# Splitting the second weight's pairs 3 to 7 inside the main loop instead of ahead of it

## The chip, the core and the metric

The kernel runs on one core of one Trainium2 chip. The metric is device time in microseconds (us), from the program's start to its end. Names used below: TensorE is PE in the profile, VectorE is DVE, ScalarE is ACT, GpSimd is POOL, SyncE is SP.

## The reference

A block-sparse attention is followed by a two-layer network with a gate. All tensors are float32.

```python
# q, k, v: 4 batches, 8 heads, 768 positions, 64 per head
scores = q @ k.T / sqrt(64)
# mask in blocks of 32: neighbours, first and last block, 3 sampled blocks per block
attn = softmax(where(mask, scores, -1e9))
x = (attn @ v) as rows: 3072 tokens x 512
h = x @ w_in                                  # 512 x 2048
g = h * erf(softplus(h))
out = g @ w_out                               # 2048 x 512
```

## The kernel before

**How the work is tiled.** Attention is cut into units: for each batch 11 "m" units of two query blocks each and 4 "f" units for the first and last block (one per pair of heads). The network works on chunks of 256 tokens in 8 groups of 256 hidden columns each; one group of one chunk is a step `m` of the main loop (line 987). In step `m`:

- TensorE does, in this order, the value products of an older unit (`values`, tile `po`), the first product of group `m` (`ff_first`, tile `h`), the scores of the newest unit (`scores`, tile `s`), and the second product of group `m - 3` (`ff_second`, tile `o`).
- ScalarE does the logarithms and squares of group `m` (`ff_logs`, tiles `x` and `y`), a first half of the attention result (`turn`), the exponentials of the newest unit (`soft_exp`: four to `pf`, then one copy to `p`), and the exponential of group `m` (`ff_exp`, `y<-y`).
- VectorE does the gate of group `m - 2` (`ff_gate`: `y<-y,h`, then the two halves of `g`), the low half of the last unit's probabilities (`soft_low`, tile `p`), the norm of the older unit (`norm`, tiles `rinv` and `xf`), the maximum of the newest unit (`soft_max`, tile `less`), the second half of the result (`turn`), and one step of the polynomial of group `m` (`ff_power`, `y<-y,x`).

Some steps carry no unit. In the first chunk, steps 0, 1, 3, 4, 5 and 6 have one, steps 2 and 7 do not. Four units have their maximum and exponentials done before the main loop's list begins, and the work before it is laid out by a scheduler; from step 3 on (`held[0] = m >= FF_LAG`, line 989) every engine runs its instructions in the order in which the code lists them. SP and POOL follow the listed order throughout.

**Buffers that couple the engines.** `h` has three PSUM buffers, so the first product of group `m` needs the gate of group `m - 3` done. `po` has one: the value products need the norm of the unit before them done. `s` has one: scores need the exponentials of the unit before done. `vn`, the scaled values of the next batch on their way to memory, has one buffer: the ScalarE instruction that fills it for the second time waits until the first transfer has left it. `qm`, the ordered queries for the "f" units, is written by VectorE in step 5 and read by the scores of step 6.

**The second weight.** All float32 factors are multiplied as two float16 halves. The second weight `w_out` lies in tile `wo` as 16 slices of 128 rows, in 8 pairs; group `fg` of the second product reads pair `fg`. Making the halves of a pair takes two instructions on ScalarE (`high`, line 466: scale and round) and then two on VectorE (`low`, line 470: what the rounding left). They are the rows `wo<-wo,sums` below. The generator `weights` (line 527) does this for pair `n - 9` in its rounds 9 to 16, all of which run before the main loop's list begins; the scheduler has laid them among the first two or three steps.

Of the kernel before, what the change touches and what calls it, by code (L numbers as in the profile page):

```python
# [31 lines left out]
def sparse_attention_moe(ctx: ExitStack, tc: tile.TileContext, qT, kT, v, sampled, w_in, w_out, out):  # L32
# [32 lines left out]
    NF = DFF // P  # L65
# [9 lines left out]
    PV_LAG = 3  # L75
    GATE_LAG = 2
    FIRST, SEEN = 6, 4
    assert NR == 3 and NB == 24 and D == 64 and H == 8

    def pick(n, share):  # L80
# [352 lines left out]
    def decode(key, i):  # L433

        first = i + APART[key]
        t = wi if key == "i" else wo
        w32 = t[:, first : first + 2, :].rearrange("p n c -> p (n c)")
        parts = [raw for n in (i, i + 1) for raw in places.pop((key, n), [])]
        mag = mags[(i // 2) % 2]
        c = 0  # L440
        for raw in parts:
            w = raw.shape[1] // 2
            raw = raw.rearrange("p (n w) -> p n w", w=2)
            lo, hi = raw[:, :, 0], raw[:, :, 1]
            m = mag[:, c : c + w]
            dve.tensor_scalar(m, hi, 3, 0x3FFFFFFF, ALU.logical_shift_left, ALU.bitwise_and)
            dve.scalar_tensor_tensor(m, hi, -0x40000000, m, ALU.bitwise_and, ALU.bitwise_or)
            done = w32[:, c : c + w].bitcast(I32)
            dve.scalar_tensor_tensor(done, lo, 29, m, ALU.logical_shift_right, ALU.bitwise_or)
            c += w  # L450

    def square(key, i):
        first = i + APART[key]
        w32 = (wi if key == "i" else wo)[:, first : first + 2, :].rearrange("p n c -> p (n c)")
        sq = mo.tile([P, 512], F32, tag="s", name=f"sq_{key}{i}", bufs=3).bitcast(BF16)
        act.activation(sq, w32, AF.Square, accum_out=wsq[key][:, i // 2 : i // 2 + 1])

    def halves(key, i):
        t, t16 = (wi, wi16) if key == "i" else (wo, wo16)
        return t[:, i + APART[key], :], t16[:, i, :512], t16[:, i, 512:]  # L460

    def scale_of(key, i):
        n = i // (2 * NK) if key == "i" else i // 2
        return (si if key == "i" else so)[:, n : n + 1]

    def high(key, i):
        w32, hi16, _ = halves(key, i)
        act.activation(hi16, w32, AF.Copy, scale=scale_of(key, i))

    def low(key, i):  # L470
        w32, hi16, lo16 = halves(key, i)
        dve.scalar_tensor_tensor(lo16, w32, scale_of(key, i), hi16, ALU.mult, ALU.subtract)
# [17 lines left out]
    def scale_pair(i):  # L490
        n = i // 2
        total = ps_o.tile([P, DM], F32, tag="o", name=f"total_{i}")[:, :1]
        pe.matmul(total, ones, wsq["o"][:, n : n + 1], start=True, stop=True)
        scale_part(total, n)

    def bound_part(part):
        return pow2_bound(wsq["i"][:, part * NK : (part + 1) * NK], f"wi{part}", True)

    def scale_half(total, part):
        scale_part(total, NP + part)  # L500
        dve.tensor_scalar(diag, eye, si[:, part : part + 1], None, ALU.mult)

    def ratios():
        dve.tensor_reduce(least[:, 0:1], si, AX.X, ALU.min)
        dve.tensor_scalar(rest_i, ii, least[:, 0:1], 2.0**-H_SHIFT, ALU.mult, ALU.mult)
        dve.tensor_reduce(least[:, 1:2], so, AX.X, ALU.min)
        for part in range(2):
            c = slice(part * NP // 2, (part + 1) * NP // 2)
            dve.tensor_scalar(ratio[:, c], io[:, c], least[:, 1:2], rest_i[:, part : part + 1], ALU.mult, ALU.mult)
        dve.tensor_scalar(least.bitcast(I32), least.bitcast(I32), -1.0, 254 * unit23, ALU.mult, ALU.add)  # L510
        dve.tensor_tensor(unscale, least[:, 0:1], least[:, 1:2], ALU.mult)
# [3 lines left out]
    def rest(i):  # L515
        rests[i] = ps_o.tile([P, DM], F32, tag="o", name=f"rest_{i}")
        pe.matmul(rests[i], diag, halves("i", i)[0], start=True, stop=False)

    def rest_low(i):
        pe.matmul(rests[i], less16, halves("i", i)[1], start=False, stop=True)  # L520

    def rest_out(i):
        act.activation(halves("i", i)[2], rests.pop(i), AF.Copy)

    assert NK * NG == NF == 16

    def weights():
        loads = {5: (("o", 0),), 6: (("o", 2),), 7: (("o", 4), ("o", 6)), 10: (("o", 8),), 11: (("o", 10),)}
        sum_i = None
        for n in range(17):  # L530
            key, i = "io"[n // 8 % 2], n % 8 * 2
            if n in (4, 9):
                with tc.high_priority():
                    scale_half(sum_i, n // 8)
            pair = None
            if 5 <= n < 9:
                pair = 2 * (n - 5)
            if 10 <= n < 14:
                pair = 2 * (n - 6)
            if pair is not None:  # L540
                for part in range(2):
                    rest(pair + part)
                    high("i", pair + part)
            if n < 16:
                decode(key, i)
            if pair is not None:
                for part in range(2):
                    rest_low(pair + part)
                    rest_out(pair + part)
            if n < 16:  # L550
                square(key, i)
            if n >= 9:
                i = 2 * (n - 9)
                scale_pair(i)
                high("o", i)
                high("o", i + 1)
                low("o", i)
                low("o", i + 1)
            for piece in loads.get(n, ()):
                load_w(*piece)  # L560
            if n in (3, 7):
                sum_i = bound_part(n // 4)
            yield
        ratios()
# [214 lines left out]
    def ff_exp(b, ch, fg):  # L779
        y = ffs[b, ch, fg][1]  # L780
        act.activation(y, y, AF.Exp, bias=C4 * C2 * C2, scale=-C4)
# [73 lines left out]
    def ahead(m):  # L855

        for c in range(1, B):
            if m - v_from[c] == 2:
                load_v(c, 1)
# [28 lines left out]
    def seen(unit):  # L888

        if unit[0] == "m":  # L890
            return unit[1], unit[2], None
        if unit[2] % 2 == 1:
            return unit[1], NU, unit[2] // 2
        return None
# [6 lines left out]
    def used_values(place):  # L901
        nonlocal vfree
        if place[2] is None:
            vfree += 2
        elif place[2] == 1:
            vfree += 3

    def unit_of(n):
        return units[n] if 0 <= n < len(units) else None
# [77 lines left out]
    for m in range(len(groups) + FF_LAG):  # L987
        ch, i = divmod(m, NGR)
        held[0] = m >= FF_LAG
        if m > FF_LAG:  # L990
            for u in range(CT):
                ff_store(*groups[m - FF_LAG - 1], u)
        steps = 0
        if ch < len(until):
            first = until[ch - 1] if ch else FIRST
            steps = int(i in spread[until[ch] - first])
        elif begun < len(units) + PV_LAG:
            steps = 1
        assert steps in (0, 1)
        group = groups[m] if m < len(groups) else None  # L1000
        last = groups[m - GATE_LAG] if GATE_LAG <= m < len(groups) + GATE_LAG else None
        unit = unit_of(begun) if steps else None
        old = unit_of(begun - PV_LAG) if steps and begun - PV_LAG >= SEEN else None
        place = seen(old) if old else None
        begun += steps
        if unit:
            ahead(begun - 1)
        if place:
            values(*place)
            used_values(place)  # L1010
        if group:
            ff_first(*group)
            ff_logs(*group)
        if steps:
            gathers()
        if unit:
            scores(unit)
            used_keys(unit)
        if m >= FF_LAG:
            for u in range(CT):  # L1020
                ff_second(*groups[m - FF_LAG], u)
        if last:
            ff_gate(*last)
        low_v()
        if open_unit:
            soft_low(open_unit)
        if place:
            norm(*place)
        if unit:
            soft_max(unit)  # L1030
        if place:
            turn(*place)
        if group:
            ff_power(*group)
        if unit:
            soft_exp(unit)
        if group:
            ff_exp(*group)
        open_unit = unit
        if unit:  # L1040
            next_queries(begun - 1)
            behind(begun - 1)
# [38 lines left out]
```

## Time and profile before

| | us |
|---|---|
| median of 3 runs | 765.58 (760.46 to 772.68) |
| profiled execution | 764.91 |
| its span | 763.1 |
| TensorE busy in the span | 686.3 (90%) |
| ScalarE busy | 591.9 (78%) |
| VectorE busy | 575.4 (75%) |
| GpSimd busy | 201.6 (26%) |

The profiled execution's own time is 1.8 us more than its span and lies between the runs. Busy time is a sum over stages that differ: the loop's first dozen steps, from about 120 to 200 us, are read below by single instructions. In these rows a time is the start from the span's beginning, then the length; a bracket gives the idle time of that engine just before and what ended it. Lengths of neighbours on one engine overlap by about a tenth of a microsecond, so a spacing of starts is a little shorter than a length.

### The profile page before, as it was taken

Reading aid. Unit: us, or ns where it says so; the run is one execution under the profiler, and the core shown is the slowest. Engines: PE = TensorE matmul, PEld = TensorE weight load, DVE = VectorE, ACT = ScalarE, POOL = GpSimd, SP = SyncE. Lnnn points to the kernel's source line nnn. Section 1 sums busy time; section 2 is a strip of 40 time slices with the busy share of each in tenths; the row PEclk is TensorE's granted clock in tenths of the full one; section 3 lists DMA queues with packets and bytes.
Section 4 is the critical chain, followed back from the end, with each engine's and each line's share of the span. In section 5 each row is a group of like instructions: output and inputs, shape, how many; then the busy total and the mean of one; then the engine's idle time right before and its main releaser. Section 6 shows DMA issues by size and latency. Waiting matters only on the chain.

```text
span 763.1 us, 24883 instructions
## 1 busy us (share of the span) xinstructions
PE 686.3 (90%) x10400; PEld 450.6 (59%) x10400; DVE 575.4 (75%) x1122; ACT 591.9 (78%) x1023; POOL 201.6 (26%) x413
## 2 busy tenths in 40 slices
PE   1336887998999999999999999999999999999997
PEld 0213554655655666666566666666666666667663
DVE  6983999978777788778687878787777786665453
ACT  2544999878877887878888887888788887776774
POOL 3026624303364313130533312033433120000000
PEclk9976998998999999999999999999999999999999
DMA  8999835896599999855997799938988677130000
GB/s 304 415 293 283 257 91 119 195 224 154 136 224 211 193 208 182 212 144 87 250 191 162 187 166 194 251 89 185 223 157 182 130 147 168 29 77 2 8 29 27
DMA packets 188048, 129.36 MB, mean 170 GB/s; under 512 B 137760, under 2 KB 160928, under 8 KB 186912
## 3 DMA queue, kind: packets, MB, share of 16 engines
q1 hardware_dynamic: 173584, 84.50, 54.1%
q10 hardware_dynamic: 8464, 25.43, 10.4%
q0 software_dynamic: 5888, 17.84, 9.6%
q8 instruction: 81, 1.33, 0.7%
q14 instruction: 31, 0.25, 0.1%
HBM read 82.81 MB, written 12.95 MB: 125 GB/s over the span
## 4 chain that ended last, share of the span: by engine, by line
PE 78%; DMA 6%; DVE 5%; ACT 5%; issue 3%; SPq 2%; ACTq 0%; DVEq 0%
PE h L48 31%; PE o L48 31%; PE s_m L48 7%; PE po_None L48 4%; PE s_f L48 3%; SPq L48 2%; DMA vbuf<-vtab 2%; DMA wo<-in_w_in_dram 2%; DMA vtab<-vn 1%; ACT x L48 1%; PE po L48 1%; DVE room L48 1%; DMA vbuf<-in_v_dram 1%; ACT pf_m L48 1%; DVE less_m L48 1%
## 5 line engine op out<-in xcount | busy, mean ns | idle before, releaser
L48 PE MATMUL h<-xT,wi 128*128 128x256 f16 x2304 | 272.3, 275 | 5.0 <-DVE y L48 4.5
L48 PE MATMUL o<-wo,g 128*128 128x512 f16 x1152 | 264.5, 379 | 0.5 <-DVE g L48 0.2
L48 PEld LDWEIGHTS <-wi 128*128 128x128 f16 x2304 | 223.7, 99 | 45.8 <-DVE y L48 4.6
L48 ACT ACTIVATE x<-x 128x512 f32<-128x512 f32 x288 | 181.6, 631 | 8.9
L48 PEld LDWEIGHTS <-g 128*128 128x128 f16 x1152 | 109.5, 98 | 127.4 <-issue 6.6
L48 POOL DMA_INDIRECT vbuf<-vtab,idx x88 | 96.5, 1097 | 185.1 <-PE po_None L48 130.3
L48 DVE SCALAR_TENSOR_TENSOR y<-y,x 128x512 f32<-128x512 f32 x96 | 67.1, 699 | 95.0 <-ACT x L48 91.6
L48 POOL COPY kbuf<-kx 128x128 f32 (+1 forms) x280 | 87.3, 357 | 94.4 <-PE s_m L48 79.8
L48 ACT ACTIVATE x<-h,isg 128x512 f32<-128x512 f32 x96 | 65.4, 682 | 49.2 <-PE h L48 31.9
L48 ACT ACTIVATE y<-y 128x512 f32<-128x512 f32 x96 | 59.7, 622 | 32.9 <-DVE y L48 32.9
L48 ACT ACTIVATE pf_m<-s_m,less_m 128x256 f32<-128x256 f32 x176 | 68.9, 473 | 19.7 <-DVE less_m L48 18.7
L48 DVE SCALAR_TENSOR_TENSOR g<-y,sums,g 128x512 f16<-128x512 f32 x96 | 73.1, 762 | 3.4
L48 DVE SCALAR_TENSOR_TENSOR y<-y,h 128x512 f32<-128x512 f32 x96 | 65.2, 679 | 0.1
L48 ACT ACTIVATE y<-x 128x512 f32<-128x512 f32 x96 | 60.4, 631 | 3.0
L48 DVE TENSOR_REDUCE less_m<-s_m 128x4 f32<-128x1024 f32 x44 | 53.6, 1218 | 11.7 <-PE s_m L48 11.6
L48 PEld LDWEIGHTS <-pT_m 128*32 128x32 f16 x3168 | 35.4, 98 | 33.9 <-issue 31.4
L48 PE MATMUL po_None<-vbuf,pT_m 128*32 128x65 f16 (+2 forms) x3168 | 41.9, 205 | 13.2 <-issue 12.5
L48 PE MATMUL s_m<-kbuf,qt 64*32 64x160 f32 x1408 | 48.2, 316 | 3.7 <-issue 2.8
L48 DVE TENSOR_SCALAR g<-y,sums 128x512 f16<-128x512 f32 x96 | 48.0, 500 | 3.4
L48 PE MATMUL s_m<-kx,qt 64*32 64x96 f32 x1408 | 31.6, 259 | 20.4 <-ACT kx L48 13.3
L48 DVE SCALAR_TENSOR_TENSOR p_m<-pf_m,p_m 128x1024 f16<-128x1024 f32 x38 | 46.4, 1221 | 0.3 <-issue 0.3
L48 DVE TENSOR_TENSOR x<-xf,x 128x256 f16<-128x256 f32 x44 | 18.8, 426 | 31.7 <-ACT x L48 31.6
(110 smaller groups left out, 609.8 us busy)
## 6 DMA issues: line engine op xcount, KB each, us to landing
vbuf<-vtab SPq DMA_DIRECT2D x80, 195.0 KB
vraw<-in_v_dram ACTq DMA_DIRECT2D x9, 768.0 KB
vtab<-vn SPq DMA_DIRECT2D x16, 390.0 KB
vbuf<-vtab SPq DMA_DIRECT2D x12, 520.0 KB
wo<-in_w_out_dram ACTq DMA_DIRECT2D x6, 1024.0 KB
qt<-in_qT_dram SPq DMA_DIRECT2D x20, 256.0 KB
kr<-in_kT_dram ACTq DMA_DIRECT2D x12, 384.0 KB
vbuf<-vtab SPq DMA_DIRECT2D x32, 130.0 KB
```

The source lines that it names most:

```text
L48: done = call(*args, **kwargs)
```

## The change

A constant `LATE = 3` divides the eight pairs. Pairs 0 to 2 are split where they were. For pairs 3 to 7 the two `high` and two `low` instructions are taken out of the generator and listed at the end of steps 4 to 8 of the main loop, behind `ff_exp` and ahead of `next_queries` and `behind`. The pair split at the end of step `m` is `m - 1`, which the second product reads in step `m + 2`. The scales of the pairs (`scale_pair`) stay in the generator. Nothing is computed more or less often.

```diff
+    LATE = 3
...
+    def convert(pair):
+        for n in (2 * pair, 2 * pair + 1):
+            high("o", n)
+        for n in (2 * pair, 2 * pair + 1):
+            low("o", n)
...
                 scale_pair(i)
-                high("o", i)
-                high("o", i + 1)
-                low("o", i)
-                low("o", i + 1)
+                if i < 2 * LATE:
+                    convert(i // 2)
...
         if group:
             ff_exp(*group)
+        if LATE <= m - 1 < NF // 2:
+            convert(m - 1)
         open_unit = unit
```

ScalarE ahead of step 3, before: from the rounding of the first weight's last slices (`wi`) to the exponential of group 0 (`y_0_0<-y_0_0`). `x_0_0` and `x_0_1` belong to groups 0 and 1, `pf_m_7` to the newest unit.

```order
L48 ACTIVATE wi<-rest_1149 128x512
L48 ACTIVATE wo<-wo,sums 128x512 x2
L48 ACTIVATE x_0_0_1417<-h_0_0_1392,isg_1390 128x512
...
L48 ACTIVATE x_0_0_1417<-x_0_0_1417 128x512
L48 ACTIVATE wo<-wo,sums 128x512 x2
L48 ACTIVATE pf_m_7_1653<-s_m_7_1601,less_m_7_1644 128x256 x2
L48 ACTIVATE x_0_1_1571<-x_0_1_1571 128x512
L48 ACTIVATE pf_m_7_1653<-s_m_7_1601,less_m_7_1644 128x256 x2
L48 ACTIVATE y_0_0_1421<-y_0_0_1421 128x512
```

The same place in the changed kernel:

```order
L48 ACTIVATE wi<-rest_1145 128x512
L48 ACTIVATE x_0_0_1397<-h_0_0_1372,isg_1370 128x512
...
L48 ACTIVATE pf_m_7_1633<-s_m_7_1581,less_m_7_1624 128x256 x4
L48 ACTIVATE y_0_1_1555<-x_0_1_1551 128x512
L48 ACTIVATE x_0_0_1397<-x_0_0_1397 128x512
L48 ACTIVATE p_m_7_1638<-pf_m_7_1633 128x4x256
L48 ACTIVATE x_0_1_1551<-x_0_1_1551 128x512
L48 ACTIVATE y_0_0_1401<-y_0_0_1401 128x512
```

Two pairs of `wo` are gone ahead of the exponential of group 0, and the copy `p_m_7` of the newest unit, which stood behind it, now stands ahead of it.

VectorE at the same place, before: `y_0_0`, `y_0_1` and `g_0_0` belong to groups 0 and 1, `p_m_7` to the newest unit.

```order
L48 TENSOR_TENSOR sums<-sums 128x1
L48 SCALAR_TENSOR_TENSOR y_0_0_1421<-y_0_0_1421,h_0_0_1392 128x512
L48 TENSOR_SCALAR g_0_0_1696<-y_0_0_1421,sums 128x512
L48 SCALAR_TENSOR_TENSOR wo<-wo,sums 128x512
L48 SCALAR_TENSOR_TENSOR g_0_0_1696<-y_0_0_1421,sums,g_0_0_1696 128x512
L48 SCALAR_TENSOR_TENSOR wo<-wo,sums 128x512
L48 SCALAR_TENSOR_TENSOR p_m_7_1658<-pf_m_7_1653,p_m_7_1658 128x4x256
L48 SCALAR_TENSOR_TENSOR wo<-wo,sums 128x512 x4
```

The same place in the changed kernel:

```order
L48 TENSOR_TENSOR sums<-sums 128x1
L48 SCALAR_TENSOR_TENSOR y_0_0_1401<-y_0_0_1401,x_0_0_1397 128x512
L48 SCALAR_TENSOR_TENSOR p_m_7_1638<-pf_m_7_1633,p_m_7_1638 128x4x256
L48 SCALAR_TENSOR_TENSOR y_0_1_1555<-y_0_1_1555,x_0_1_1551 128x512
L48 SCALAR_TENSOR_TENSOR y_0_0_1401<-y_0_0_1401,h_0_0_1372 128x512
L48 TENSOR_SCALAR g_0_0_1676<-y_0_0_1401,sums 128x512
L48 SCALAR_TENSOR_TENSOR g_0_0_1676<-y_0_0_1401,sums,g_0_0_1676 128x512
```

All the `wo` rows have left this place (ten in the whole stretch), and `p_m_7` and the step of group 1 stand ahead of the gate of group 0.

VectorE and ScalarE at the end of step 4, in the changed kernel, VectorE first (from the maximum of unit 9 to the gate of group 3), then ScalarE (from the exponentials of unit 9 to group 5):

```order
L48 TENSOR_REDUCE less_m_9_2078<-s_m_9_2019 128x4
L48 TENSOR_SCALAR less_m_9_2078<-less_m_9_2078 128x4
L48 TENSOR_TENSOR x_0_6_2081<-xf_6_2074,x_0_6_2081 128x256
L48 SCALAR_TENSOR_TENSOR y_0_4_1993<-y_0_4_1993,x_0_4_1989 128x512
L48 SCALAR_TENSOR_TENSOR wo<-wo,sums 128x512 x2
L48 TENSOR_REDUCE vmax_1641<-vraw_1_1684 128x1
L48 TENSOR_REDUCE top_v_2099<-vmax_1641 128x1
L48 SCALAR_TENSOR_TENSOR y_0_3_1788<-y_0_3_1788,h_0_3_1759 128x512
```

```order
L48 ACTIVATE pf_m_9_2086<-s_m_9_2019,less_m_9_2078 128x256 x4
L48 ACTIVATE p_m_9_2091<-pf_m_9_2086 128x4x256
L48 ACTIVATE y_0_4_1993<-y_0_4_1993 128x512
L48 ACTIVATE wo<-wo,sums 128x512 x2
L48 DMA kr_0_2103<-in_kT_dram 128x768
L48 ACTIVATE x_0_5_2203<-h_0_5_2178,isg_1370 128x512
```

Only the `wo` rows are new at this place; without them the rows of before are the same in the same order. Steps 5, 6, 7 and 8 take theirs at the same point. The lists of POOL and SP are unchanged.

## Rows read from the trace of the kernel before

**Rows 1.** Part 1 of the page: busy time, share, instructions.

```profile
PE 686.3 (90%) x10400; PEld 450.6 (59%) x10400; DVE 575.4 (75%) x1122; ACT 591.9 (78%) x1023; POOL 201.6 (26%) x413
```

**Rows 2.** Stretches: window, length, PE, PEld, DVE, ACT, POOL, granted clock, DMA, GB/s.

```profile
120.00:130.00 10.00, 6.72 (x89) 4.65 (x90) 9.13 (x20) 10.00 (x20) 1.75 (x3) 0.66 0.36 80
...
300.00:500.00 200.00, 198.59 (x3027) 132.20 (x3020) 157.91 (x301) 167.53 (x287) 51.95 (x111) 1.00 0.90 185
```

**Rows 3.** Timeline of TensorE, steps 3, 4, 6 and 9: start, length, instruction.

```profile
123.28 5.30 PE L48 MATMUL h<-xT,wi 128*128 128x256 f16 x24 [4.50 <-DVE y L48]
...
129.82 2.76 PE L48 MATMUL o<-wo,g 128*128 128x512 f16 x12
134.39 0.88 PE L48 MATMUL po_None<-vbuf,pT_m 128*32 128x65 f16 x72 [1.80 <-issue]
135.21 2.79 PE L48 MATMUL h<-xT,wi 128*128 128x256 f16 x24
...
150.00 0.89 PE L48 MATMUL po_None<-vbuf,pT_m 128*32 128x65 f16 x72 [0.68 <-DVE xf L48]
...
174.72 1.50 PE L48 MATMUL po_None<-vbuf,pT_m 128*32 128x65 f16 x72 [4.18 <-issue]
176.15 4.72 PE L48 MATMUL h<-xT,wi 128*128 128x256 f16 x24
```

**Rows 4.** Instructions that touch `wo`, 112 to 132 us: nanoseconds min/median/max.

```profile
L48 DVE SCALAR_TENSOR_TENSOR wo<-wo,sums x10: 741/752/803, 115.0 to 129.8; 128x512 f16<-128x512 f32 x10
L48 ACT ACTIVATE wo<-wo,sums x9: 750/769/785, 111.4 to 129.0; 128x512 f16<-128x512 f32 x9
```

**Rows 5.** Timeline of VectorE: norm of unit 5, in step 3.

```profile
133.74 0.55 DVE L48 TENSOR_REDUCE xf<-po_None 128x192 f32<-128x384 f32 x1
```

**Rows 6.** Timeline of ScalarE: one pair's `high`; ends of steps 4 to 7.

```profile
118.64 1.36 ACT L48 ACTIVATE wo<-wo,sums 128x512 f16<-128x512 f32 x2
...
145.59 0.61 ACT L48 ACTIVATE y<-y 128x512 f32<-128x512 f32 x1
146.11 0.67 ACT L48 ACTIVATE x<-h,isg 128x512 f32<-128x512 f32 x1
...
154.70 0.61 ACT L48 ACTIVATE y<-y 128x512 f32<-128x512 f32 x1
...
162.49 0.61 ACT L48 ACTIVATE y<-y 128x512 f32<-128x512 f32 x1
...
171.67 0.63 ACT L48 ACTIVATE y<-y 128x512 f32<-128x512 f32 x1 [0.83 <-DVE y L48]
```

**Rows 7.** Timeline of VectorE, steps 4 to 8: gates, and what follows each power.

```profile
137.00 0.68 DVE L48 SCALAR_TENSOR_TENSOR y<-y,h 128x512 f32<-128x512 f32 x1
...
143.80 1.75 DVE L48 TENSOR_REDUCE vmax<-vraw 128x1 f32<-128x1536 f32 x1
...
145.66 0.68 DVE L48 SCALAR_TENSOR_TENSOR y<-y,h 128x512 f32<-128x512 f32 x1
...
152.89 0.58 DVE L48 COPY qm<-qt 64x256 f32<-64x256 f32 x2
...
154.01 0.68 DVE L48 SCALAR_TENSOR_TENSOR y<-y,h 128x512 f32<-128x512 f32 x1
...
161.58 0.68 DVE L48 SCALAR_TENSOR_TENSOR y<-y,h 128x512 f32<-128x512 f32 x1
...
166.82 1.22 DVE L48 SCALAR_TENSOR_TENSOR vn<-vraw,s_v,vn 128x384 f16<-128x384 f32 x2 [3.25 <-ACT vn L48]
...
171.56 0.68 DVE L48 SCALAR_TENSOR_TENSOR y<-y,h 128x512 f32<-128x512 f32 x1
```

**Rows 8.** Two transfers out of `vn`: SP's issue and who waited for the landing.

```profile
157.12 0.36 SPq L48 DMA_DIRECT2D vtab<-vn  x1
...
166.11 1.12 ACT L48 ACTIVATE vn<-vraw,s_v 128x384 f16<-128x384 f32 x2 [3.01 <-DMA vtab<-vn]
...
168.10 0.36 SPq L48 DMA_DIRECT2D vtab<-vn  x1
...
172.57 0.25 POOL L48 MEMSET vn<- 128x24 f16 x1 [1.47 <-DMA vtab<-vn]
```

## The prediction

> **What bounds the kernel now.** I read the page's busy times first, then a table of stretches, then the timelines of TensorE, VectorE and ScalarE over 110 to 200 us. Over the whole span TensorE is busy 90% [rows 1], and from 300 to 500 us it is busy 198.6 of 200 us [rows 2]: there TensorE is the end, nothing in the change touches it, and a delay of TensorE before 200 us is carried nearly whole to the end. So the change is worth what it does to TensorE's arrival at about step 10.
>
> The reader should see three holes in TensorE in the loop's first steps [rows 3]. The first product of step 3 starts after 4.50 us idle that VectorE's gate of group 0 ended, and runs 5.30 us, twice its later 2.79. The value products of step 4 start after 1.80 us idle; the profile gives no releaser, but the norm of unit 5 frees their only buffer and its reading of `po` ends at 133.74 + 0.55 = 134.29 [rows 5], 0.10 before the start at 134.39. Third, 4.18 us idle before step 9's value products at 174.72, again behind a late norm: VectorE had stood 3.25 us for ScalarE's `vn`, and ScalarE 3.01 us for the transfer that left `vn` [rows 7, 8].
>
> **What the change removes.** Ten ScalarE and ten VectorE instructions of 0.77 and 0.75 us [rows 4] (the sample shows nine of ScalarE's, the trace misses one) leave the stretch 111 to 131 us; with the overlap of neighbours that is about 6.2 us of ScalarE and 6.6 of VectorE. What it buys:
>
> - Step 3's start. Two of ScalarE's pairs (2.5 us) stood ahead of the exponential of group 0, but the copy `p_m_7` (about 1.0) now stands there, and on VectorE `p_m_7` (1.1) and the step of group 1 (0.7) now stand ahead of the gate. Laying ScalarE's list out from 110.95 I get `p_m_7` ready at 120.5, then 1.1 + 0.7 + 0.7 on VectorE: the gate is done at about 123.0 instead of 123.2. Gain 0.3 us; the slow first product stays, since TensorE stands idle as long.
> - Step 4's start. VectorE no longer has eight `low` ahead of the norm of unit 5, which ends near 128.6, while TensorE's `o` of step 3 ends at 129.82 + 2.76 - 0.3 = 132.3. The 1.80 us hole closes. TensorE enters step 4 at 132.3 instead of 134.39: **gain 2.1 us**.
> - VectorE's own lead is larger: the maximum of unit 8 can start with its scores at 129.6 instead of behind the backlog at 134.6, less a new wait of 0.8 for ScalarE. Its gate of step 4 comes at 132.9 instead of 137.00 [rows 7]: a lead of 4.1.
>
> **What it adds.** Two instructions on each of ScalarE and VectorE per step look cheap. The place makes them dear. In the new order VectorE's two `low` stand right behind `y<-y,x`, and each waits for ScalarE's `high`, which stands behind four exponentials, the copy `p` and the exponential of the group. All of VectorE's list behind them waits too: the next gate, `soft_low`, the norm. I read the stall off the rows of before, as if the pair stood there, with 1.3 us for two `high` [rows 6] and 0.7 for the last `low` [rows 4]:
>
> - Step 4: ScalarE's exponential is done at 146.11 [rows 6]; 146.11 + 1.3 + 0.7 = 148.1, where VectorE went on at 143.80 [rows 7]. 4.3 us, of which 1.3 is work.
> - Step 5: 154.70 + 0.5 + 2.0 = 157.2 against 152.89: 4.3 us.
> - Step 6: 162.49 + 0.5 + 2.0 = 165.0 against 161.58: 3.4 us.
> - Step 7: 171.67 + 0.5 + 2.0 = 174.2 against 171.56: 2.6 us.
> - Step 8: the same kind, but behind it stands the norm for a value product of step 12, since steps 10 and 11 have none; cost nothing. If that cover is gone it costs up to 2.6.
>
> Now the running balance of VectorE against the rows of before. It enters step 4 with 4.1 in hand; 0.6 goes to a wait for ScalarE, whose logarithms lead only by TensorE's 2.1; the stall takes 4.3: 0.8 behind at the gate of 145.66. About 0.3 comes back in the norm of unit 7, which ran slow before. Step 6's value products, 150.00 before, come at about 150.7 while TensorE is ready at 147.3: a new hole of some 3.4 us, and the gain of 2.1 is gone. Step 5's stall makes it 4.6 to 4.8 behind at 154.01, and `qm` (152.89 to 153.5 before) comes at about 158, so step 6's scores wait as well. Step 6's stall makes it 8.0 behind at 161.58; but the next instruction had waited 3.25 us [rows 7], so the delay there is 4.7 again.
>
> The transfer from `vn` decides the next bit. It was issued at 157.12 and let ScalarE go on at 166.11, 9.0 us; another, at 168.10, was gone by 172.57, 4.5 us [rows 8]. The issue moves to about 161.8. With 9.0 us ScalarE passes it at 170.8, with 4.5 at once behind its `high`, at 168.9. Group 7's logarithms follow, and VectorE's step on them (170.88 before) is 4.1 or 2.6 late; with step 7's stall of about 2.5 the norm of unit 9 and step 9's value products are **6.6 or 5.1 late**. The shorter transfer is the nearer, as fewer loads are left ahead of it: I take 5.5, and keep both. From step 10 on TensorE waits for nothing new: the gates it needs come 3 us or more before it. Pair 3's halves are ready near 145 and read near 159, so the weights themselves are never late. SP and POOL keep their lists; their waits on VectorE move with it.
>
> Sum: 5.5, less about 0.5 that holes of TensorE after 200 us may take back (bounds 0 and 1), is +5 on the profiled execution's 764.9: **770 us**. That execution lies 0.7 below the median of the runs.
>
> **The clock.** The new hole before step 6 is 3.4 us. After the 4.50 us hole the granted clock is 0.66 as the mean of 120 to 130 us [rows 2], a mixture of its two levels of 1.2 and 2.4 GHz. After 1.80 us idle the next first product ran at 2.79, after 4.18 at 4.72, with the value products at 1.50 instead of 0.89 [rows 3]. So it costs 0 to 2.5 us of TensorE; nearest is the row of 4.18, 2.5. In my sum it lies under VectorE's stall: step 6's scores wait for `qm` until 158, and a slow `h` ends at 157.
>
> The Trainium skill ("TensorE: Matmul & The Clock Gate", section on HAM oscillation) says that waits between bursts of matmuls drop the engine to half clock, and that every burst then pays again. By that rule both new holes, before step 6's value products and before its scores, would be paid in full: 775 us. The trace agrees after 4.18 us; no row shows it at 3.4.
>
> **The rivals.**
>
> - *The stalls stay covered.* If ScalarE, relieved too, gets its `high` done early, VectorE's lead of 4.1 and TensorE's slack could cover the stalls of steps 4 and 5, and the 2.1 us gain stays: 764.9 - 2.1 = 762.8, faster. It decides itself at step 6's value products: before 148 it has won. For it: both engines have 6 us less behind them. Against: ScalarE cannot start `pf` before VectorE's maximum, so relief ahead does not shorten the stall. Chance 0.14.
> - *A draw.* The late stalls (steps 6 and 7) hide wholly under the `vn` wait and later holes take back a microsecond or two: 4.7 - 2.5 to 4.7 - 1, so 766 to 768. Chance 0.20.
> - *Both new holes are exposed at half clock* as reckoned above: 2 x 2.5 us more, 775. Against: the rows put this time under VectorE. Chance 0.06.
> - *The clock stays at half through steps 6 to 10*, and TensorE, not VectorE, sets the pace: `h` 4.72, `o` 2 x 2.75, scores 2 x 1.3, value products 1.50 make 14.3 us a step against VectorE's 12.2 between the new gates of steps 5 and 6, some 2 us in five steps: 770 + 10 = 780, and worse where it lasts. It needs the holes to recur before the clock is back. Against: after the 4.50 us hole one `h` paid and `o` at 129.82 ran at full speed. Chance 0.04.
>
> My own case, 768 to 773, has 0.56. The predicted time is its middle, 770. The range takes in most of the fast case and the exposed holes, and the runs' own spread: 762 to 777. A change under 2% (15 us) cannot be told from none here. No case but the last comes near it: faster by over 2% 0.02, within 2% 0.94, slower by over 2% 0.04.
>
> **What would show it.** Right: VectorE idle 2 to 3 us ahead of `wo` in steps 4 to 6, ended by ScalarE's `wo`; no hole before step 4's value products, which start near 132; a hole of about 3 us before step 6's, near 151; step 9's 5 to 7 us later than 174.72; steps after 200 us of the same length. Wrong: step 6's value products before 148, or `wo` on VectorE without idle time ahead of it, or a first product of step 3 that starts two or more microseconds earlier, which would move everything behind it.

## The result and the profile after

The change made the kernel slower: 775.69 us (median of 20 runs, 770.42 to 780.77) against 765.83 (20 runs of before beside them), ratio 1.0138 with a 95% interval of [1.0115, 1.0161]. Forecast was 770; the median lies inside the range, but the loss is 9.9 us where 4 to 5 were forecast. A ratio leaves out the few runs that fell into a slower state of the chip, so here and below it need not equal the quotient of two medians.

The profiled execution of the change took 780.46, span 778.6; it is one of the long ones. Its busy times are those of [rows 1] within about 2 per cent, but TensorE's share fell, as the span is longer (part 1 of the page):

```profile
PE 694.5 (89%) x10400; PEld 454.1 (58%) x10400; DVE 575.7 (74%) x1122; ACT 592.2 (76%) x1023; POOL 197.3 (25%) x413
```

TensorE's timeline, answering to [rows 3]:

```profile
129.93 4.26 PE L48 MATMUL h<-xT,wi 128*128 128x256 f16 x24 [4.84 <-DVE y L48]
...
135.26 2.76 PE L48 MATMUL o<-wo,g 128*128 128x512 f16 x12
137.96 0.88 PE L48 MATMUL po_None<-vbuf,pT_m 128*32 128x65 f16 x72
...
156.48 1.20 PE L48 MATMUL po_None<-vbuf,pT_m 128*32 128x65 f16 x72 [3.41 <-DVE xf L48]
157.61 4.08 PE L48 MATMUL h<-xT,wi 128*128 128x256 f16 x24
164.50 2.90 PE L48 MATMUL s_f<-kx,qm 128*128 128x512 f32 x4 [2.81 <-DVE qm L48]
...
186.84 0.89 PE L48 MATMUL po_None<-vbuf,pT_m 128*32 128x65 f16 x72 [2.62 <-issue]
...
206.88 2.91 PE L48 MATMUL o<-wo,g 128*128 128x512 f16 x12 [1.80 <-ACT wi L48]
```

Step 3's first product starts 6.65 us later than in [rows 3]. That belongs to this execution and not to the change: in three later profiles of the change this row stands at 121.86, 123.37 and 122.79, and in two more of before at 122.32 and 121.71. So all marks below are counted from the start of this row. Then the reader sees the 1.80 us hole of step 4 gone (8.03 behind the mark, 11.11 before), two new holes in step 6 (3.41 and 2.81), step 9's value products at 56.91 against 51.44, and a wait in step 11, 1.80 for ScalarE's `wi`, that no row of before has. Step 11's `o` before:

```profile
193.72 2.75 PE L48 MATMUL o<-wo,g 128*128 128x512 f16 x12
```

VectorE's timeline, the last power step ahead of the first pair and the five pairs:

```profile
145.62 0.69 DVE L48 SCALAR_TENSOR_TENSOR y<-y,x 128x512 f32<-128x512 f32 x1
148.96 1.42 DVE L48 SCALAR_TENSOR_TENSOR wo<-wo,sums 128x512 f16<-128x512 f32 x2 [2.65 <-ACT wo L48]
...
162.44 1.41 DVE L48 SCALAR_TENSOR_TENSOR wo<-wo,sums 128x512 f16<-128x512 f32 x2 [2.98 <-ACT wo L48]
...
174.63 1.42 DVE L48 SCALAR_TENSOR_TENSOR wo<-wo,sums 128x512 f16<-128x512 f32 x2 [2.08 <-ACT wo L48]
...
182.35 1.41 DVE L48 SCALAR_TENSOR_TENSOR wo<-wo,sums 128x512 f16<-128x512 f32 x2 [1.31 <-ACT wo L48]
...
191.31 1.41 DVE L48 SCALAR_TENSOR_TENSOR wo<-wo,sums 128x512 f16<-128x512 f32 x2 [2.16 <-ACT wo L48]
```

VectorE stands 2.65 + 2.98 + 2.08 + 1.31 + 2.16 = 11.2 us for ScalarE's `wo`, in front of 1.4 us of work each time. ScalarE at the first of these, in step 9 and in step 11:

```profile
147.70 0.61 ACT L48 ACTIVATE y<-y 128x512 f32<-128x512 f32 x1
148.22 1.32 ACT L48 ACTIVATE wo<-wo,sums 128x512 f16<-128x512 f32 x2
...
197.22 0.42 ACT L48 ACTIVATE x<-xf 128x256 f16<-128x256 f32 x1 [1.77 <-DVE xf L48]
...
206.16 0.67 ACT L48 ACTIVATE wi<-o,iso 128x512 f32<-128x512 f32 x1
```

The `high` stands right behind the group's exponential, as the list has it. The row at 197.22 is `turn`, which waits for VectorE's norm of unit 10. The last row is the copy of the first chunk's finished rows out of `o`; until it is done, step 11's `o` has no buffer.

### The profile page after: what moved, and what is told of

Its sections match the earlier page's. It is cut to its first block, busy times and chain, and to the rows that moved or that the text cites. A ratio compares the mean times of both kernels' runs of the same rounds, so it can differ in the third digit from the quotient of the medians.

```text
span 778.6 us, 24883 instructions
## 1 busy us (share of the span) xinstructions
PE 694.5 (89%) x10400; PEld 454.1 (58%) x10400; DVE 575.7 (74%) x1122; ACT 592.2 (76%) x1023; POOL 197.3 (25%) x413
## 4 chain that ended last, share of the span: by engine, by line
PE 70%; DMA 9%; DVE 7%; ACT 7%; SPq 3%; issue 3%; ACTq 0%; DVEq 0%
PE h L48 28%; PE o L48 28%; PE s_m L48 6%; PE po_None L48 4%; DMA vbuf<-vtab 3%; SPq L48 3%; ACT x L48 2%; PE s_f L48 2%; DMA wo<-in_w_in_dram 2%; DMA wo<-in_w_out_dram 2%; DMA vtab<-vn 1%; DVE y L48 1%; ACT y L48 1%; ACT pf_m L48 1%; PE po L48 1%
## 5 line engine op out<-in xcount | busy, mean ns | idle before, releaser
L48 PE MATMUL o<-wo,g 128*128 128x512 f16 x1152 | 267.9, 383 | 2.3 <-ACT wi L48 2.0
L48 POOL COPY kbuf<-kx 128x128 f32 (+1 forms) x280 | 83.7, 345 | 93.7 <-PE s_m L48 79.6
L48 PE MATMUL s_m<-kbuf,qt 64*32 64x160 f32 x1408 | 50.4, 318 | 4.4 <-issue 3.7
```

The source lines that it names most:

```text
L48: done = call(*args, **kwargs)
```

## The experiments

The kernels of one group ran on the same chip. The median of before differs from group to group (759 to 769 us), so times and ratios are set against the before of the same group.

**Where the low stands (first group).** Theory: the loss is VectorE's wait for `high`. Rivals: the work itself, or the loads behind `high` on ScalarE's queue.

*Low in the next step.* The `high` stay; only the `low` move behind the next gate (`highs` and `lows_of` are the two halves of `convert`):

```diff
             ff_gate(*last)
+        if LATE <= m - 2 < NF // 2:
+            lows_of(m - 2)
...
-            convert(m - 1)
+            highs(m - 1)
```

> The two high of a pair stay at the end of steps 4 to 8 as in the change; its two low move into the next step, right behind VectorE's gate, so that VectorE does not stand for ScalarE. Wait theory (the loss is VectorE standing 2 to 3 us per step for high): no idle time ahead of wo on VectorE, step 6's value products less than 1 us after TensorE is ready, 763 to 768 us, ratio to before 0.995 to 1.003. Work theory (the loss is 2.6 us per step more work on two engines that are nearly full): ScalarE and VectorE still fall behind TensorE, 771 to 776 us, ratio 1.007 to 1.014. Queue theory (the loss is what stands behind high on ScalarE's queue, the key loads of the next batch): as in the change, 773 to 777 us.

Measured: 764.57 against 768.59, ratio 0.9946 [0.9911, 0.9982], just past the fast end of the wait theory's 0.995 to 1.003. VectorE (three of five pairs) and TensorE in step 6:

```profile
144.78 1.41 DVE L48 SCALAR_TENSOR_TENSOR wo<-wo,sums 128x512 f16<-128x512 f32 x2
...
154.04 1.41 DVE L48 SCALAR_TENSOR_TENSOR wo<-wo,sums 128x512 f16<-128x512 f32 x2
...
177.52 1.41 DVE L48 SCALAR_TENSOR_TENSOR wo<-wo,sums 128x512 f16<-128x512 f32 x2 [0.17 <-ACT wo L48]
```

```profile
149.79 0.88 PE L48 MATMUL po_None<-vbuf,pT_m 128*32 128x65 f16 x72
```

No wait above 0.17 us, no hole, though the same work is done in these steps and ScalarE's list is the change's word for word. The work and the queue are out as causes.

*High first.* The `high` stand behind the logarithms, ahead of the unit's exponentials; the `low` where the change has them:

```diff
             ff_logs(*group)
+        if LATE <= m - 1 < NF // 2:
+            highs(m - 1)
...
-            convert(m - 1)
+            lows_of(m - 1)
```

> The two high of a pair stand right behind the logarithms of the same step, ahead of the exponentials of the unit; the low stay where the change has them. Wait theory: VectorE finds them done, idle ahead of wo under 0.5 us, but the exponentials of each unit start up to 1.3 us later, so a part remains: 765 to 770 us, ratio 0.999 to 1.006. Work theory: 771 to 776 us. Queue theory: the key loads are still behind two high, 773 to 777 us.

Measured: 0.9971 [0.9933, 1.0008], a little below the wait theory's 0.999 to 1.006 and far from the other two. VectorE no longer waits ahead of `wo`, but a hole of 2.42 us is left before step 6's value products, as that theory has it for the delayed exponentials:

```profile
149.77 0.89 PE L48 MATMUL po_None<-vbuf,pT_m 128*32 128x65 f16 x72 [2.42 <-DVE xf L48]
```

*Next batch first.* The split goes to the very end of the step:

```diff
-        if LATE <= m - 1 < NF // 2:
-            convert(m - 1)
...
             behind(begun - 1)
+        if LATE <= m - 1 < NF // 2:
+            convert(m - 1)
```

> The whole split of a pair stands at the very end of its step, behind the next batch's loads, maximum, scaling and the ordering of the queries. Wait theory: the 1.9 us of the maximum in step 4 and the 1.1 us of queries and scales in step 5 now run while VectorE would stand; about 3 us back and step 6's scores no longer wait for the queries: 770 to 773 us, ratio 1.006 to 1.010. Queue theory: the key loads and the next batch's values leave ScalarE 1.3 us earlier in each step, and nearly all comes back: 766 to 768 us. Work theory: as in the change, 774 to 777 us.

Measured: 775.89 us, 1.0094 [1.0060, 1.0129]. The ratio is the wait theory's (1.006 to 1.010), the time the work theory's (774 to 777), and the change itself has ratios from 1.0091 to 1.0138 below; so the total decides nothing, and the rows have to. VectorE, steps 4 to 6:

```profile
143.36 1.42 DVE L48 SCALAR_TENSOR_TENSOR wo<-wo,sums 128x512 f16<-128x512 f32 x2 [0.80 <-ACT wo L48]
...
156.49 1.41 DVE L48 SCALAR_TENSOR_TENSOR wo<-wo,sums 128x512 f16<-128x512 f32 x2 [2.95 <-ACT wo L48]
168.57 1.41 DVE L48 SCALAR_TENSOR_TENSOR wo<-wo,sums 128x512 f16<-128x512 f32 x2 [3.09 <-ACT wo L48]
```

In step 4 the maximum covers all but 0.80 of the wait. In steps 5 and 6 nothing does: ScalarE's `vn` now stands ahead of the `high` as well.

*The quiet step.* Pairs 3 and 4 ahead of the loop, the rest in step 7:

```diff
-    LATE = 3
+    LATE = 5
...
-        if LATE <= m - 1 < NF // 2:
-            convert(m - 1)
+        if m == 7:
+            for pair in range(LATE, NF // 2):
+                convert(pair)
```

> Pairs 3 and 4 are split ahead of the loop as before, pairs 5, 6 and 7 together at the end of step 7, which carries no unit. Wait theory: six low fewer ahead of the norm of unit 5, so the hole before step 4's value products closes (1.8 us), and the 4 us on each engine in step 7 lie mostly under the waits for the transfer out of the scaled values: 763 to 767 us, ratio 0.996 to 1.001. Work theory: the same 4 us on both engines delay the norm of unit 9 and step 9's value products by about as much: 767 to 770 us. Queue theory: step 8's loads are 4 us late: 768 to 772 us.

Measured: 769.11 us, 1.0025 [0.9993, 1.0057]. The wait theory's figure was missed, and the time lies in the work theory's 767 to 770. The rows show waits that neither theory had. ScalarE, and TensorE in step 8:

```profile
168.36 1.32 ACT L48 ACTIVATE wo<-wo,sums 128x512 f16<-128x512 f32 x2
169.89 1.38 ACT L48 ACTIVATE wo<-wo,sums 128x512 f16<-128x512 f32 x2 [0.21 <-DVE wo L48]
171.43 1.38 ACT L48 ACTIVATE wo<-wo,sums 128x512 f16<-128x512 f32 x2 [0.16 <-DVE wo L48]
```

```profile
169.12 0.38 PE L48 MATMUL o<-wo,g 128*128 128x512 f16 x1 [2.21 <-ACT wo L48]
169.91 4.22 PE L48 MATMUL o<-wo,g 128*128 128x512 f16 x11 [0.41 <-DVE wo L48]
```

The halves of a pair are written over the raw slices of the pair before it, so the three pairs take turns; and step 8's `o` reads pair 5 and now waits for it. The place was quiet, but it was too late. How much of the total these waits make was not tried.

**Which pairs cost what (second group).** The stall of pair 7 in step 8 was costed at nothing. One kernel moves the `low` of pair 7 alone (shown), another those of pairs 3 to 6 alone (with the two conditions exchanged):

```diff
+        if LATE <= m - 2 < NF // 2 and m - 2 == 7:
+            lows_of(m - 2)
...
-            convert(m - 1)
+            highs(m - 1)
+            if m - 1 < 7:
+                lows_of(m - 1)
```

> As the change, but pair 7's two low (step 8) move behind the gate of step 9; pairs 3 to 6 keep their stalls. Step-8 theory (step 8's stall was costed at nothing and delays the norm of unit 10, ScalarE's logarithms and the copies of the first finished rows out of o): the wait of step 11's o for ScalarE's copy (1.80 us in the change) is gone, and 2 to 4 us with what follows it: ratio to before 1.004 to 1.009. Rival (the step-8 stall is covered, and the late loss comes from the delay of step 9 alone): as the change, ratio 1.010 to 1.015.

Measured: 1.0101 [1.0054, 1.0148]. Step 11's wait is gone, but nothing is gained against the change in the same group (1.0095, below): in the total this is the rival's figure.

> The other half: pairs 3 to 6 have their low behind the next step's gate, only pair 7 keeps its stall in step 8. Step-8 theory: about 2 to 4 us are lost against the kernel with all low moved: ratio to before 0.997 to 1.002. Rival: nothing is lost, 0.992 to 0.997.

Measured: 0.9991 [0.9957, 1.0025], the step-8 theory's figure, but the interval takes in the rival's as well, and the kernel with all five moved had run in another group.

*From pair 2.* All `low` moved, and `LATE = 2`:

> All low moved behind the next gate, and pair 2 goes into the loop as well (step 3). If the relief ahead of the loop still shortens the wait of step 3's first product for the gate of group 0 (4.8 to 5.0 us): up to 1.3 us faster than with five pairs, ratio 0.991 to 0.995. If that gate is bound by the copies and logarithms that remain there: the same, 0.993 to 0.998; VectorE has 1.3 us more in step 4.

Measured: 0.9979 [0.9951, 1.0007]. TensorE, steps 3, 5 and 6:

```profile
119.95 2.79 PE L48 MATMUL h<-xT,wi 128*128 128x256 f16 x24 [1.92 <-DVE y L48]
...
137.22 0.89 PE L48 MATMUL po_None<-vbuf,pT_m 128*32 128x65 f16 x72 [1.82 <-DMA vbuf<-vtab]
...
148.20 0.89 PE L48 MATMUL po_None<-vbuf,pT_m 128*32 128x65 f16 x72 [3.53 <-DVE xf L48]
```

The big hole before step 3 shrinks from about 5 us to 1.92 and the product runs at full speed, more than expected. Holes in steps 4 to 6 take it back, one of them for a transfer of the values; in step 6 VectorE's norm sets the pace.

> The change itself once more, beside its variants. Ratio to before 1.010 to 1.016. Its profile, counted from the first product of step 3, shows what of the first profile was the execution and what the kernel: step 9's value products 56 to 58 us behind it (before 51.4), the end 646 to 650 (before 639.8); the first product itself near 124 instead of 129.9 if the late start of the profiled execution was chance, near 130 if the change delays it.

Measured: 1.0095 [1.0058, 1.0131]; step 9 at 56.87, the end at 640.54, the first product at 121.86. So the late start of the first profile was chance, and step 9 is reproduced to 0.04 us. The ratio lies just under the 1.010 expected, and the end misses its 646 to 650 by over 5 us; more of this at the end of the next section.

**How far two executions of one kernel differ (third group).** No edits.

> The kernel before, against itself: ratio 0.997 to 1.003. Its profile gives the marks on this chip: step 9's value products 51 to 52 us behind the first product of step 3, step 11's o at 70 to 71, step 18's first product at 124 to 125.

> The kernel before once more, one look: how far the marks differ between two executions of the same kernel. If by less than 1 us up to step 11 and by more behind it, the part of the loss that lies behind step 11 is partly chance of the execution.

Measured: 0.9997 [0.9955, 1.0040] for the first. Its marks missed what was expected: 49.73 for step 9 and 66.18 for step 11's `o`. TensorE in step 9, of the first:

```profile
172.05 0.88 PE L48 MATMUL po_None<-vbuf,pT_m 128*32 128x65 f16 x72 [2.54 <-issue]
```

The hole of 4.18 us in [rows 3] is 2.54 here and 2.11 in the second profile. VectorE's wait for `vn` ahead of it, 3.25 us in [rows 7], first and second profile:

```profile
164.23 1.22 DVE L48 SCALAR_TENSOR_TENSOR vn<-vraw,s_v,vn 128x384 f16<-128x384 f32 x2 [1.68 <-ACT vn L48]
```

```profile
164.50 1.22 DVE L48 SCALAR_TENSOR_TENSOR vn<-vraw,s_v,vn 128x384 f16<-128x384 f32 x2 [2.11 <-ACT vn L48]
```

> The change on the same chip. Ratio 1.009 to 1.014. If all of the loss is made by step 9, the marks behind step 3's first product are 5 to 6 us late from step 9 to the end. If step 8's stall and the late start of the second batch add to it, 5 to 6 at step 9, 6 to 7 at step 11's o, 7 to 9 at step 18 and at the end.

Measured: 1.0133 [1.0082, 1.0185].

> All five pairs with their low behind the next step's gate, again, on the chip of the two looks at before: ratio 0.992 to 0.998; step 9's value products 48 to 49 us behind step 3's first product, against 51 to 52 before and 56 to 58 in the change.

Measured: 0.9974 [0.9940, 1.0008]; step 9 came at 50.14, later than expected. The marks from the groups in which before takes 766 to 769 us, in us behind step 3's first product:

| | step 9 `po` | step 11 `o` | step 18 `h` | end |
|---|---|---|---|---|
| before, three profiles | 51.44, 49.73, 51.14 | 70.44, 66.18, 69.32 | 124.47, 122.96, 125.52 | 639.82, 639.98, 642.69 |
| change, two profiles | 56.91, 57.25 | 76.95, 77.24 | 132.44, 134.04 | 648.67, 651.53 |
| low in the next step, two | 48.32, 50.14 | 67.48, 68.20 | 121.84, 124.79 | 637.19, 641.88 |

In means the change is 6.3 us late at step 9, 8.4 at step 11, 8.9 at step 18 and 9.3 at the end. By these means the loss is made in two places and not given back; but the three profiles of before differ among themselves by 1.7 us at step 9 and by 4.3 at step 11, so the parts are known no better than that.

The second place shows more sharply when the time is counted from step 9's value products to step 11's `o`, over all groups: it is 19.81 to 20.04 us in the six profiles in which pair 7 stalls (four of the change, two with the `low` of pairs 3 to 6 moved) and 17.93 to 19.16 in the six in which all `low` or pair 7's alone stand in the next step. The means are 1.7 us apart.

**The four cells on one chip (fourth group).**

> Pairs 3 to 6 stall as in the change, pair 7 has its low behind the next gate; the four cells of pairs 3 to 6 by pair 7 now share one chip. Step-8 theory: 2 us or more below the change (0.003 in the ratio). Second-batch theory (what is lost behind step 9 follows from the delay made by pairs 3 to 6, because keys, values and transposes of the second batch start that much later): within 1 us of the change.

> Pairs 3 to 6 behind the next gate, pair 7 stalls. Step-8 theory: 2 us or more above the kernel with all five moved. Second-batch theory: within 1 us of it.

> All five pairs behind the next gate, third time: ratio 0.993 to 0.998.

> The change, fourth time: ratio 1.009 to 1.014; step 9's value products 56 to 58 us behind step 3's first product, step 11's o at 76 to 78.

| before 759.03 | pair 7 stalls | pair 7's low in the next step |
|---|---|---|
| pairs 3 to 6 stall | 765.26, 1.0091 [1.0052, 1.0130] | 763.17, 1.0074 [1.0042, 1.0105] |
| pairs 3 to 6 in the next step | 758.78, 0.9995 [0.9965, 1.0025] | 756.43, 0.9987 [0.9954, 1.0021] |

Pairs 3 to 6 cost 6.5 and 6.7 us by the medians, 0.0096 and 0.0087 of the ratio. Pair 7 costs 2.1 and 2.4 by the medians, 0.0017 and 0.0008 by ratios whose intervals overlap. TensorE in step 11 with all stalls, then with the stall of pair 7 alone, then with all but that one:

```profile
200.29 2.91 PE L48 MATMUL o<-wo,g 128*128 128x512 f16 x12 [2.79 <-ACT wi L48]
```

```profile
194.33 2.91 PE L48 MATMUL o<-wo,g 128*128 128x512 f16 x12 [0.51 <-ACT wi L48]
```

```profile
196.34 2.90 PE L48 MATMUL o<-wo,g 128*128 128x512 f16 x12
```

With pair 7 moved that wait is absent, whatever pairs 3 to 6 do. So step 8's stall is what makes ScalarE late for the copy out of `o`: shown for the wait, and for the 1.7 us up to step 11's `o`. In the total it is not shown: about 2 us by the medians of this group, within their noise, only 1.3 and 0.6 by its ratios, and nothing in the second group. All five moved missed its 0.993 to 0.998 by a little.

## Why the prediction was right in its mechanism and wrong in its size

- **Removal.** Right. The first product of step 3 kept its hole (4.84 us) and stayed slow (4.26 us at a granted clock of 0.64, where 2.79 is its length at full clock), and the hole of step 4 closed. That this is a gain by itself shows where the `low` do not stall: 0.9946, 0.9974 and 0.9987, one of three intervals clear of 1, by 4.1, 2.0 and 1.0 us where about 2 were forecast.
- **The stalls.** Right in cause, place and size: idle 2.65, 2.98 and 2.08 us ahead of `wo` where 3.0, 3.0 and 2.1 were forecast beside the work, ended by ScalarE; step 6's value products 26.55 us behind the mark (forecast 150.7 against 123.0, 27.7), then the wait for `qm`.
- **The `vn` transfer.** The shorter landing was the right choice: the transfer issued at 168.00 let POOL go on at 172.52, 4.5 us later, and ScalarE passed `vn` at 175.11 with no wait. Step 9 came 5.5 us late against the execution that the sum started from (56.91 against 51.44), as taken.
- **The clock.** Right: after 3.41 us idle `h` took 4.08 us (granted clock 0.68 from 156.40 to 161.70), and it lay under the wait for `qm` (2.81 us), so it was not paid. The scores and `o` behind that wait were slow as well (2.90 and 4.40 us against 1.46 and 2.75 in step 8), but step 9's value products still stood 2.62 us for the norm, so that was covered too. By the Trainium skill ("TensorE: Matmul & The Clock Gate", section on HAM oscillation) a long enough wait between bursts of matmuls drops the clock, and each burst behind such a wait pays again. The rows of step 6 agree; in step 9 of the change in the fourth group a hole of 3.36 us left `h` at 2.79. The rival that added the half-clock bursts in full named 775 us; it is near the median for another reason.
- **Step 8, "cost nothing".** This step failed. Only the value products were asked for as a cover; the other customer of VectorE's late norm was overlooked. ScalarE's `turn` of unit 10 waits for it (1.77 us in the change), then group 10's logarithms, then the copy out of `o`, and step 11's `o` stands 1.80 to 2.79 us in the four profiles of the change. The price written beside it, up to 2.6 "if that cover is gone", is the nearer one at step 11: 2.1 in the means of the table (6.3 to 8.4), 1.7 between the profiles with and without this stall.
- **"From step 10 on TensorE waits for nothing new", and 0.5 us given back.** Failed with it. In the means of the table nothing comes back from step 11 to the end: another 0.8 us is lost.
- **The base.** The sum let 3.25 us of VectorE's delay (8.0 to 4.7) lie in its wait for `vn`. That was the longest of three: 1.68 and 2.11 in the other profiles of before, with holes of 2.54 and 2.11 at step 9 instead of 4.18. So this term was too large for a usual execution, and against the mean of three profiles step 9 is 6.3 late, not 5.5.

So where 5.5 - 0.5 = 5 stood, the means of the table give 6.31 + 2.14 + 0.82 = 9.27 us for the delay up to step 9, up to step 11 and behind it, and 9.9 was measured in the medians of the result.

Open: this holds for the groups where before takes 766 to 769 us, with ratios of 1.0138 and 1.0133. Where before takes 759 to 762 the ratio is 1.0095 and 1.0091, the loss by the medians 6.1 and 6.2 us, not far from the 5 forecast. The intervals overlap, so a part may be chance; and the chip alone does not decide it, as the second and the third group bear the same chip number. The change's marks at steps 9 and 11 are the same within 0.9 us in both kinds of group (57.59 and 77.50 in the fourth), but its end is 8 to 11 us nearer in the second and the fourth (640.54 and 640.61). One difference stands in the profiles of every kernel, before included: TensorE's scores `s_m` stop 15 to 21 times for nothing that the profile shows in the groups where before is slow, 3 to 6 times in the others. No profile of before was taken in the second and fourth group, so whether this makes the loss larger was not tried.

## What to carry to other kernels

When a producer on one in-order engine and its consumer on another are listed together, the consumer's place is set by when the producer's whole list lets it run, not by how long either takes: 1.4 us of work held VectorE for another 1.3 to 3.0 us, five times. Put the consumer where the producer is surely done, here behind the next gate, and the same move turns from a loss of 1% into no loss or a small gain. And follow a delay to every customer of the late result, up to the buffer that is freed last, before costing it at nothing.

## What the runs showed of the hardware that was not expected

- Whether the matmuls behind a hole ran slow did not follow from the hole's length alone. In step 9, `h` took 4.46 us after a hole of 2.11 (before, second profile of the third group; granted clock 0.69 from 172.80 to 178.30), but 2.79 after 2.54 (before, the first of that group), after 3.03 (high first) and after 3.36 (the change, fourth group; granted clock 1.00 from 180.30 to 184.00), and 4.46 again after 3.58 (pair 7 moved, fourth group).
- One list of instructions reached step 3 at 121.86, 122.79, 123.37 and 129.93 us in four profiles of the change. That spread of 8 us is nearly as much as the whole effect, so one profile's span says little here; marks counted from an instruction say more.
